# Attention scores of six batches on four 64 by 64 squares of TensorE instead of two 128 by 64 halves

## Chip, cores and metric

The kernel runs on one core of a Trainium2 chip (trn2). The metric is the device time of one execution in microseconds (us); lower is better. The time before is the median of three runs.

## What is computed

Windowed causal attention with a linear position bias, and behind it a bilinear feed-forward layer over all tokens:

```python
# q, k, v: (8, 8, 576, 64); w_a, w_b: (512, 1536); w_out: (1536, 512); float32
scores = q @ k.T / sqrt(64)                    # per batch and head
mask = (rel >= 0) & (rel < 128)                # rel = query position - key position
scores = where(mask, scores - slope[head] * abs(rel), -1e9)
attn = softmax(scores) @ v
x = attn with heads joined                     # (8 * 576, 512)
out = ((x @ w_a) * (x @ w_b)) @ w_out
```

## The kernel before

Everything is float32 outside; inside, each large product is made of float16 halves. A value x becomes hi = fp16(x) and lo = fp16(x - hi), and a product of two such values is three float16 matmuls (hi hi, hi lo, lo hi) that add up in PSUM. The feed-forward layer takes most of TensorE's time: up (w_a and w_b; line 941 of the helper `terms`) and down (w_out; line 1102), as matmuls of 128 rows by 128 columns of the array with 288 columns streamed. From the third batch on it multiplies blocks by a seven-product scheme.

While the feed-forward of one batch runs, the attention of the next is woven into it. `attention()` (a generator) makes one step per pair of heads, 4 pairs per batch (p = 0 to 3), and yields seven times in a step; `Pace` advances it along the feed-forward steps. TensorE's order is written out by this weave and is kept; the orders of the other engines are set by the scheduler that builds the program. Pairs p = 2 and 3 fall into the up phase of the feed-forward, p = 0 and 1 into the down phase.

**Scores.** Queries go in 9 tiles of 64. Tile i needs 64, 128 or 192 keys (64 for tile 0, 128 for tile 1, 192 for the other seven). Batch 0 and batch 1 make their scores in float32 (lines 646 and 445). For the batches 2 to 7 (six of them, 24 pairs of heads) `lay_out_qk` first sends four copies from SBUF to SBUF: `qst` gets q-hi in partitions 0 to 63 and q-lo in 64 to 127, and then k-hi and k-lo are doubled into both partition halves, over the place of q. `scores` (line 449) then makes, per tile and head, two matmuls over 128 partitions: qst times k-hi (hi hi + lo hi) and qst times k-lo (hi lo + lo lo). The two heads of the pair sit in the two column halves of the array (PSUM partitions 0 to 63 and 64 to 127). The profile writes this shape as 128*64.

**Banks.** `BANKS` puts the 9 tiles into four PSUM banks of 512 columns, 3 + 2 + 2 + 2 tiles, each 384 columns wide in all. They come from the pool `ps_at`, which has 3 banks in rotation and also serves the attention's second product (`pv`, `x_ps`, line 575, 42 matmuls in 128*64, two banks) and small sums (`qtot`, `vtot`). A step calls `scores` for banks 0 and 1 together, then bank 2, then bank 3.

**Behind a bank.** Per tile VectorE adds the bias and takes the row minimum (line 454, which reads PSUM), ScalarE takes the exponential (line 455). `normalize` later makes reciprocals of the sums (467, 468) and writes the normalised probabilities as hi (ScalarE, 471) and lo (VectorE, 472) into `phl`. A transposing DMA makes `pT` of it, which `pv` reads one or two steps later. `keep_x` (488) moves the result of `pv` to SBUF, `split_x` (509, 510) makes halves of it for the feed-forward.

## Time and profile before

| | |
|---|---|
| median of the runs | 968.81 us (968.03 to 969.47) |
| the profiled execution's own time | 967.01 us |
| its span, first to last instruction | 965.2 us |
| TensorE busy | 951.8 us, 9304 matmuls |
| VectorE, ScalarE, GpSimd busy | 723.0, 636.7, 260.7 us |
| granted TensorE clock | 0.998 of 2.4 GHz |

The profiled execution is 1.80 us under the median. Busy time of TensorE counts a matmul from its start to a modelled end; successive matmuls overlap, so the distance between two starts says what a matmul takes in a stream. In the timeline a row joins equal instructions that follow each other: its first number is the start of the first, its second the time to the end of the last.

### The profile page before, as it was taken

Reading aid. Unit: us, or ns where it says so; the run is one execution under the profiler, and the core shown is the slowest. Engines: PE = TensorE matmul, PEld = TensorE weight load, DVE = VectorE, ACT = ScalarE, POOL = GpSimd, SP = SyncE. Lnnn points to the kernel's source line nnn. Section 1 sums busy time; section 2 is a strip of 40 time slices with the busy share of each in tenths; the row PEclk is TensorE's granted clock in tenths of the full one; section 3 lists DMA queues with packets and bytes.
Section 4 is the critical chain, followed back from the end, with each engine's and each line's share of the span. In section 5 each row is a group of like instructions: output and inputs, shape, how many; then the busy total and the mean of one; then the engine's idle time right before and its main releaser. Section 6 shows DMA issues by size and latency. Waiting matters only on the chain.

```text
span 965.2 us, 23861 instructions
## 1 busy us (share of the span) xinstructions
PE 951.8 (99%) x9304; PEld 743.2 (77%) x9305; DVE 723.0 (75%) x2004; ACT 636.7 (66%) x1725; POOL 260.7 (27%) x307
## 2 busy tenths in 40 slices
PE   8989999999999999999999999999999999999998
PEld 6667777777877777777877777777777777877776
DVE  7999997578888768887876677767676676589860
ACT  6877787577776666776766766767667666424531
POOL 1211222045546123632432122401222112311110
PEclk9999999999999999999999999999999999999999
DMA  9373745626437333464246452473245441210001
GB/s 357 144 271 106 261 83 127 163 85 120 89 92 173 76 69 70 108 165 94 45 100 178 88 114 50 101 190 82 57 95 111 137 75 39 51 38 7 2 7 43
DMA packets 148433, 102.83 MB, mean 107 GB/s; under 512 B 120032, under 2 KB 128352, under 8 KB 147296
## 3 DMA queue, kind: packets, MB, share of 16 engines
q1 hardware_dynamic: 138816, 91.77, 38.7%
q10 hardware_dynamic: 9504, 9.54, 3.1%
q8 instruction: 73, 1.20, 0.5%
q14 instruction: 40, 0.33, 0.1%
HBM read 48.33 MB, written 9.44 MB: 60 GB/s over the span
## 4 chain that ended last, share of the span: by engine, by line
PE 84%; DVE 6%; ACT 4%; DMA 3%; issue 1%; SPq 1%; ACTq 0%; POOL 0%; DVEq 0%
PE dn_ps L1102 22%; PE ch L941 19%; PE up_ps L941 15%; PE p L941 14%; PE x_ps L575 4%; PE sc_ps L449 4%; PE dch L1127 2%; PE d L1127 1%; DMA v<-in_vP 1%; DMA qk<-in_kT 1%; DVE wsum L146 1%; ACT t L455 1%; DMA wdn<-in_w_b 1%; ACT vsq L341 1%; PE sc_ps L445 1%
## 5 line engine op out<-in xcount | busy, mean ns | idle before, releaser
L941 PEld LDWEIGHTS <-wup 128*128 128x128 f16 x3072 | 296.1, 98 | 83.9 <-issue 7.9
L1102 PE MATMUL dn_ps<-h,wdn 128*128 128x288 f16 x1728 | 218.4, 286 | 0.0
L1102 PEld LDWEIGHTS <-wdn 128*128 128x128 f16 x1728 | 165.8, 98 | 44.7
L941 PE MATMUL up_ps<-xr,wup 128*128 128x288 f16 x1536 | 195.5, 286 | 2.2 <-DVE v L704 1.1
L941 PEld LDWEIGHTS <-wsum 128*128 128x128 f16 x1152 | 111.7, 98 | 30.9 <-issue 1.3
L1056 POOL TENSOR_TENSOR xr<-xr,row 128x288 f32<-128x288 f32 x64 | 63.0, 985 | 265.7 <-DVE row L1054 234.0
L455 ACT ACTIVATE t<-t,mn 128x192 f32<-128x192 f32 (+2 forms) x252 | 107.2, 427 | 25.7 <-DVE mn L454 25.4
L472 DVE SCALAR_TENSOR_TENSOR phl<-t,rin,phl 128x192 f16<-128x192 f32 (+2 forms) x252 | 103.8, 453 | 17.7 <-ACT phl L471 17.6
L941 PE MATMUL ch<-xr,wup 128*128 128x288 f16 x768 | 115.0, 286 | 0.3 <-DVE xr L1061 0.3
L941 PE MATMUL p<-xr,wup 128*128 128x288 f16 x768 | 115.1, 286 | 0.0
L941 PE MATMUL ch<-xr,wsum 128*128 128x288 f16 x768 | 111.5, 286 | 0.4 <-ACT xr L1026 0.4
L471 ACT ACTIVATE phl<-t,rin 128x192 f16<-128x192 f32 (+2 forms) x252 | 88.9, 425 | 30.3 <-DVE rin L468 15.7
L933 ACT CAST h<-xr 128x576 f16<-128x576 f32 x84 | 56.0, 667 | 46.9 <-DVE xr L1061 23.2
L454 DVE CUSTOM_DVE_ANT_0 t<-sc_ps,bias,neg 128x192 f32<-128x192 f32 (+2 forms) x216 | 73.7, 390 | 10.7 <-PE sc_ps L449 10.6
L934 DVE TENSOR_TENSOR h<-xr,h 128x576 f16<-128x576 f32 x78 | 61.5, 790 | 24.6 <-ACT h L933 24.2
L510 DVE TENSOR_TENSOR xr<-v,xr 128x576 f16<-128x576 f32 x52 | 48.8, 951 | 24.2 <-ACT xr L509 24.1
L430 POOL TENSOR_SCALAR bias<-rel_sb,ninv,sl_sb 128x192 f32<-128x192 f32 x24 | 22.5, 936 | 148.5 <-DVE mn L454 125.0
L1038 ACT ACTIVATE row<-ch,g 128x288 f32<-128x288 f32 x64 | 31.8, 497 | 45.3 <-PE ch L941 45.3
L941 PE MATMUL p<-xr,wsum 128*128 128x288 f16 x384 | 57.5, 286 | 0.0
L455 ACT ACTIVATION_READ_ACCUMULATOR t<-t,mn 128x1 f32 x252 | 47.5, 189 | 0.0
L504 POOL TENSOR_TENSOR xq<-xq,sq 128x576 bf16<-128x576 bf16 x21 | 29.0, 1379 | 66.2 <-ACT sq L503 66.2
L1061 DVE SCALAR_TENSOR_TENSOR xr<-xr,g,ch 128x288 f32<-128x288 f32 x64 | 32.6, 510 | 15.0 <-PE ch L941 15.0
(193 smaller groups left out, 1497.7 us busy)
## 6 DMA issues: line engine op xcount, KB each, us to landing
v<-in_vP SPq DMA_DIRECT2D x8, 1280.0 KB, 6.3
qk<-in_qT SPq DMA_DIRECT2D x28, 288.0 KB, 4.0
qk<-in_kT SPq DMA_DIRECT2D x28, 288.0 KB, 4.4
out<-row ACTq DMA_DIRECT2D x56, 144.0 KB, 2.4
wdn<-in_w_a SPq DMA_DIRECT2D x12, 512.0 KB, 5.2
wdn<-in_w_b SPq DMA_DIRECT2D x12, 512.0 KB, 6.0
wdn<-in_w_out SPq DMA_DIRECT2D x12, 512.0 KB, 5.0
qst<-qkh SPq DMA_DIRECT2D x24, 144.0 KB, 2.8
```

The lines of the kernel that those rows point to most:

```text
L449: pe.matmul(ps[64 * e:64 * e + 64, c:c + w], o.qs[:, e, qq], ks[:, e, kk], start=not last, stop=last)
L454: beside[1] = vec.tensor_tensor_reduce(out=t[:, c:c + w], in0=ps[:, c:c + w], in1=o.bias[:, WIN - w:WIN], scale=-0.125 if o.b == 1 else o. ...
L455: beside[0] = act.activation(t[:, c:c + w], t[:, c:c + w], AF.Exp, bias=o.mn[:, n:n + 1], scale=-1.0, accum_out=o.sm[:, n:n + 1])
L471: beside[0] = last_phl[0] = act.activation(phl[:, 0, pc:pc + w], e, AF.Copy, scale=s)
L472: beside[1] = vec.scalar_tensor_tensor(out=phl[:, 1, pc:pc + w], in0=e, scalar=s, in1=phl[:, 0, pc:pc + w], op0=ALU.mult, op1=ALU.subtract)
L510: vec.tensor_tensor(out=xs[:, n, 1, :, :], in0=src, in1=xs[:, n, 0, :, :], op=ALU.subtract)
L575: last = pe.matmul(xp[oc // 512][64 * h:64 * h + 64, o0:o0 + w], vt[0:rows, c:c + 64], probs(pt, rows, blocks, h), start=(n == 0 and first ...
L933: act.copy(h[:, f, :, 0, :], hid)
L934: eng.tensor_tensor(out=h[:, f, :, 1, :], in0=hid, in1=h[:, f, :, 0, :], op=ALU.subtract)
L941: pe.matmul(ps[:, 0:HT], w[:, wi, k, :], xs[:, b, xi, k, :], start=(first and n == 0), stop=(last and n == len(ks) - 1), skip_group_check= ...
L1056: pool.tensor_tensor(out=x0, in0=x0, in1=mid, op=ALU.mult)
L1102: pe.matmul(ps[:, 0:HT], wdn[:, f, wi, e * P:(e + 1) * P], h[:, f, t, hi, :], start=(m == 0 and n == 0), stop=(m == NF - 1 and n == 2))
```

## The change

`BANKS` no longer serves the batches 2 to 7. `FOLDED` puts their 9 tiles into two groups of two banks. A group's first bank is computed in the upper half of the array's rows (partitions 0 to 63 of the operands), its second bank in the lower half (64 to 127), each head in its column half as before, so four squares of 64 by 64 hold a matmul each. `in_turn` orders the two banks' matmuls by the columns that each half has been given so far. Per tile and head there are three matmuls (hi hi, lo hi, hi lo); lo lo is no longer computed. The copies change with it: the row half that holds q gets k-hi and k-lo of the keys 0 to 319 beside it, the half that holds k gets q-hi and q-lo of the queries 320 to 575, and nothing is overwritten. A step calls `score_pair` twice, where banks 0 and 1, and bank 2, stood; `pv` of p = 0 and 3 moves behind the next yield; for p = 2 `normalize` runs once over nine tiles.

```diff
--- before.py
+++ after.py
@@ -40,6 +40,24 @@
 
 BANKS = (((0, 0), (1, 128), (8, 256)), ((2, 0), (3, 320)), ((4, 0), (5, 320)), ((6, 0), (7, 320)))
 NCOL = 2048
+
+
+FOLDED = ((((2, 0), (1, 192), (0, 320)), ((5, 0), (6, 320))), (((3, 0), (4, 320)), ((7, 0), (8, 320))))
+FOLD = 320
+
+
+def in_turn(g):
+
+    ends, todo, out = [0, 0], [[(i, c, n) for i, c in FOLDED[g][half] for n in range(3)] for half in range(2)], []
+    while any(todo):
+        half = min((h for h in range(2) if todo[h]), key=lambda h: ends[h])
+        i, c, n = todo[half].pop(0)
+        out.append((half, i, c, n))
+        ends[half] += TILES[i][1]
+    return out
+
+
+ORDER = [in_turn(g) for g in range(2)]
 PRIO = 2000
 SEVEN = B - 1
 
@@ -413,11 +431,10 @@
 
 
         b, p, hi, lo, sc = o.b, o.p, o.kh, o.kl, o.sc
-        o.qs = work.tile([P, 2, S], F16, tag="qst", name="qst", bufs=1)
-        sp.dma_start(o.qs[0:64, :, :], hi[0:64, :, :])
-        sp.dma_start(o.qs[64:128, :, :], lo[0:64, :, :])
-        sp.dma_start(hi[0:64, :, :], hi[64:128, :, :])
-        sp.dma_start(lo[0:64, :, :], lo[64:128, :, :])
+        o.other = work.tile([P, 2, 2, FOLD], F16, tag="qst", name="qst", bufs=1)
+        for n, x in enumerate((hi, lo)):
+            sp.dma_start(o.other[0:64, n, :, :], x[64:128, :, 0:FOLD])
+            sp.dma_start(o.other[64:128, n, :, 0:S - FOLD], x[0:64, :, FOLD:S])
 
         t = small.tile([P, 1], F32, tag="ninv", name="ninv")
         vec.scalar_tensor_tensor(out=t, in0=sc[:, 0:1], scalar=-8.0, in1=sc[:, 1:2], op0=ALU.mult, op1=ALU.mult)
@@ -444,10 +461,10 @@
                         r = slice(64 * e, 64 * e + 64)
                         pe.matmul(ps[r, c:c + w], o.q[r, qq], o.k[r, kk], start=True, stop=True)
                 continue
-            for ks, last in ((o.kh, False), (o.kl, True)):
-                for e in range(2):
-                    pe.matmul(ps[64 * e:64 * e + 64, c:c + w], o.qs[:, e, qq], ks[:, e, kk], start=not last, stop=last)
-        for i, c in BANKS[bi]:
+        minima_of(o, BANKS[bi], ps, t, ready)
+
+    def minima_of(o, tiles, ps, t, ready):
+        for i, c in tiles:
             pc, w = TILES[i]
             n = o.n
             with tc.issue_after(ready.ins) if ready else ExitStack():
@@ -455,6 +472,22 @@
             beside[0] = act.activation(t[:, c:c + w], t[:, c:c + w], AF.Exp, bias=o.mn[:, n:n + 1], scale=-1.0, accum_out=o.sm[:, n:n + 1])
             o.parts.append((n, t[:, c:c + w], pc, w))
             o.n += 1
+
+    def score_pair(o, g, ready=None):
+
+        banks_of = [(ps_at.tile([P, 512], F32, tag="at", name="sc_ps"), work.tile([P, 512], F32, tag="t", name="t", bufs=4)) for _ in range(2)]
+        order = ORDER[g]
+        for half, i, c, n in order:
+            w = TILES[i][1]
+            qq, kk = slice(64 * i, 64 * i + 64), slice(64 * i + 64 - w, 64 * i + 64)
+            r = slice(64 * half, 64 * half + 64)
+            mine, other = (o.kh, o.kl), o.other
+            a, z = ((0, 0), (1, 0), (0, 1))[n]
+            for e in range(2):
+                qx, kx = (mine[a][r, e, qq], other[r, z, e, kk]) if half == 0 else (other[r, a, e, 64 * i - FOLD:64 * i + 64 - FOLD], mine[z][r, e, kk])
+                pe.matmul(banks_of[half][0][64 * e:64 * e + 64, c:c + w], qx, kx, start=(n == 0), stop=(n == 2))
+        for half, (ps, t) in enumerate(banks_of):
+            minima_of(o, FOLDED[g][half], ps, t, ready)
 
     def normalize(o):
 
@@ -785,8 +818,10 @@
             if two == 2 and p == 1:
                 with behind():
                     nxt = squares(i + 1)
-            for bi in range(two if o else 0):
-                scores(o, bi, nxt.ready if two == 2 and p == 1 and nxt else None)
+            if o and two == 2:
+                score_pair(o, 0, nxt.ready if p == 1 and nxt else None)
+            elif o:
+                scores(o, 0)
             if two == 1 or p != 1:
                 with behind():
                     nxt = squares(i + 1)
@@ -815,24 +850,22 @@
             if p != 2:
                 split(nxt, p != 3)
             yield i + 3 / 7
-            if o:
+            if o and two == 2:
+                score_pair(o, 1)
+            elif o:
                 scores(o, 2)
             if p == 3 and nxt and nxt.b > 1:
                 low_qk(nxt, beside[1])
-            if prev and p not in (1, 2):
+            if two == 1 and prev and p not in (1, 2):
                 pv(prev.p, st, prev, prev.vhl)
-            if two == 2 and p in (1, 3):
-                if p == 2:
-                    with behind():
-                        normalize(o)
-                scores(o, 3)
             yield i + 4 / 7
+            if two == 2 and prev and p not in (1, 2):
+                pv(prev.p, st, prev, prev.vhl)
             if p == 2:
                 prev.vhl = split_v(st, prev.p)
-                if two == 1 or p not in (1, 3):
-                    with behind():
-                        normalize(o)
-            if o and (two == 1 or p not in (1, 3)):
+                with behind():
+                    normalize(o)
+            if o and two == 1:
                 scores(o, 3)
             lay_out(nxt)
             load(i + 2)
@@ -844,7 +877,7 @@
                 for k, _ in enumerate(split_x(st, b - 1 <= 3, b - 1 >= 2)):
                     yield i + (4.2 + 0.2 * k) / 7
             yield i + 5 / 7
-            if o:
+            if o and o.parts:
                 with behind():
                     normalize(o)
             if p == (0 if b == 1 else 1):
```

TensorE, second run of scores of pair p = 0 in the first batch whose scores follow this path (sc_ps are the PSUM tiles, qst the copies, qkh and qkl the hi and lo halves). Before:

```order
L449 LDWEIGHTS qst_2233
L449 MATMUL sc_ps_2486<-qkh_2028,qst_2233 64x192
L449 LDWEIGHTS qst_2233
L449 MATMUL sc_ps_2486<-qkh_2028,qst_2233 64x192
L449 LDWEIGHTS qst_2233
L449 MATMUL sc_ps_2486<-qkl_2029,qst_2233 64x192
L449 LDWEIGHTS qst_2233
L449 MATMUL sc_ps_2486<-qkl_2029,qst_2233 64x192
```

The same place in the changed kernel:

```order
L488 LDWEIGHTS qkh_2028
L488 MATMUL sc_ps_2496<-qst_2233,qkh_2028 64x192
L488 LDWEIGHTS qkh_2028
L488 MATMUL sc_ps_2496<-qst_2233,qkh_2028 64x192
L488 LDWEIGHTS qst_2233
L488 MATMUL sc_ps_2498<-qkh_2028,qst_2233 64x192
L488 LDWEIGHTS qst_2233
L488 MATMUL sc_ps_2498<-qkh_2028,qst_2233 64x192
L488 LDWEIGHTS qkl_2029
L488 MATMUL sc_ps_2496<-qst_2233,qkl_2029 64x192
L488 LDWEIGHTS qkl_2029
L488 MATMUL sc_ps_2496<-qst_2233,qkl_2029 64x192
```

Before, one bank is filled, and each weight load and matmul stands twice, once per head; now two banks take turns, two heads each, with the operands' places exchanged between the row halves.

ScalarE, in an up phase of the seven-product scheme, pair p = 2 (t are the exponentials, phl the normalised probabilities, ch and p the feed-forward's PSUM tiles, xr and row what they are copied to). Before:

```order
L1038 ACTIVATE row<-ch,g 128x288
L1044 COPY xr<-p_8686 128x288
L467 ACTIVATE rin<-sm 128x7
L471 ACTIVATE phl<-t,rin 128x64
L471 ACTIVATE phl<-t,rin 128x128
L471 ACTIVATE phl<-t,rin 128x192 x5
L933 CAST h<-xr 128x2x288
L455 ACTIVATE t,sm<-t,mn 128x192 x2
L1026 COPY xr<-ch 128x288
```

The same place in the changed kernel:

```order
L472 ACTIVATE t,sm<-t,mn 128x192 x4
L1071 ACTIVATE row<-ch,g 128x288
L1077 COPY xr<-p_8964 128x288
L500 ACTIVATE rin<-sm 128x9
L504 ACTIVATE phl<-t,rin 128x192
L504 ACTIVATE phl<-t,rin 128x128
L504 ACTIVATE phl<-t,rin 128x64
L504 ACTIVATE phl<-t,rin 128x192 x6
L966 CAST h<-xr 128x2x288
L1059 COPY xr<-ch 128x288
```

Before, seven tiles are normalised and two exponentials follow ahead of the next copy of ch; now four exponentials stand ahead, and nine tiles are normalised in one piece.

## Rows read from the trace of the kernel before

**Rows 1.** The page's first part: busy time of each engine and its share of the span.
```profile
span 965.2 us, 23861 instructions
PE 951.8 (99%) x9304; PEld 743.2 (77%) x9305; DVE 723.0 (75%) x2004; ACT 636.7 (66%) x1725; POOL 260.7 (27%) x307
```
**Rows 2.** The page's chain that ended last, by engine.
```profile
PE 84%; DVE 6%; ACT 4%; DMA 3%; issue 1%; SPq 1%; ACTq 0%; POOL 0%; DVEq 0%
```
**Rows 3.** Timeline of TensorE, banks 0 and 1 (p = 0): start, length, engine, line, shapes.
```profile
608.62 0.90 PE L1102 MATMUL dn_ps<-h,wdn 128*128 128x288 f16 x6
609.45 0.22 PE L449 MATMUL sc_ps<-qkh,qst 128*64 128x64 f16 x2
609.50 0.20 PE L449 MATMUL sc_ps<-qkl,qst 128*64 128x64 f16 x2
609.53 0.23 PE L449 MATMUL sc_ps<-qkh,qst 128*64 128x128 f16 x2
...
609.65 0.25 PE L449 MATMUL sc_ps<-qkh,qst 128*64 128x192 f16 x2
...
610.06 0.25 PE L449 MATMUL sc_ps<-qkl,qst 128*64 128x192 f16 x2
610.24 4.58 PE L1102 MATMUL dn_ps<-h,wdn 128*128 128x288 f16 x36
```
**Rows 4.** Timeline of TensorE, p = 0: bank 2 with pv, then bank 3 alone.
```profile
614.69 3.10 PE L1102 MATMUL dn_ps<-h,wdn 128*128 128x288 f16 x24
...
618.07 1.51 PE L575 MATMUL x_ps<-pT,vhl 128*64 128x128 f16 x42
619.52 2.38 PE L1102 MATMUL dn_ps<-h,wdn 128*128 128x288 f16 x18
...
622.28 5.32 PE L1102 MATMUL dn_ps<-h,wdn 128*128 128x288 f16 x42
```
**Rows 5.** Timeline of TensorE around banks 2 and 3 of p = 1.
```profile
635.96 3.10 PE L1102 MATMUL dn_ps<-h,wdn 128*128 128x288 f16 x24
...
639.77 5.44 PE L1102 MATMUL dn_ps<-h,wdn 128*128 128x288 f16 x43
```
**Rows 6.** Timeline of TensorE around banks 0, 1 and vtot of p = 2.
```profile
649.34 0.90 PE L941 MATMUL ch<-xr,wup 128*128 128x288 f16 x6
...
651.07 0.90 PE L941 MATMUL p<-xr,wup 128*128 128x288 f16 x6
```
**Rows 7.** Timeline of TensorE around a pv that runs alone.
```profile
679.88 0.90 PE L941 MATMUL ch<-xr,wsum 128*128 128x288 f16 x6
680.71 1.54 PE L575 MATMUL x_ps<-pT,vhl 128*64 128x128 f16 x42
682.18 0.91 PE L941 MATMUL p<-xr,wsum 128*128 128x288 f16 x6
```
**Rows 8.** Timeline of TensorE around bank 2, pv and bank 3 of p = 3.
```profile
700.20 0.90 PE L941 MATMUL ch<-xr,wup 128*128 128x288 f16 x6
...
703.16 0.91 PE L941 MATMUL p<-xr,wup 128*128 128x288 f16 x6
```
**Rows 9.** Timeline of TensorE, a bank of batch 1: float32 in two squares.
```profile
133.08 0.17 PE L112 MATMUL wtot<-c,ones 128*128 128x1 bf16 x1
133.18 0.87 PE L445 MATMUL sc_ps<-qkl,qkh 64*64 64x192 f32 x8
133.98 1.03 PE L941 MATMUL up_ps<-xr,wup 128*128 128x288 f16 x7
```
**Rows 10.** TensorE's waits: line waited for, us in total, times, longest us.
```profile
PE sc_ps L449 <- DVE mn L454: 0.6, 1, 0.6
...
PE ch L941 <- ACT xr L1026: 0.4, 2, 0.2
```
**Rows 11.** ScalarE's groups by shape: count, busy us, mean ns, idle before.
```profile
L455 ACT ACTIVATE t<-t,mn 128x192 f32<-128x192 f32 x196 | 86.9, 445 | 11.5 <-DVE mn L454 11.4
L471 ACT ACTIVATE phl<-t,rin 128x192 f16<-128x192 f32 x196 | 73.6, 442 | 10.9 <-DVE rin L468 10.9
```
**Rows 12.** The page's DMA issues: KB each, us from issue to landing.
```profile
qst<-qkh SPq DMA_DIRECT2D x24, 144.0 KB, 2.8
...
qkl<-qkl SPq DMA_DIRECT2D x24, 144.0 KB, 2.5
```

## Prediction

> **What bounds the kernel.** I read the page's first part, then the chain that ended last, then the timeline of TensorE around each kind of attention work, then its waits. The first shows TensorE busy for 99% of the span and the next engine for 75% [rows 1]. The chain is 84% TensorE [rows 2]. That it passes through other engines for the rest stops the stream little: the waits of the scores and of the seven products' ch, the two that matter below, are 0.6 and 0.4 us in the whole kernel [rows 10]. So time taken out of TensorE's stream comes out of the total, as long as no new wait opens.
>
> The timeline gives each stop of the feed-forward a price: from the start of its last matmul before to that of the first behind, less one normal step. That step is 0.12 us, from 36 matmuls in one row: (4.58 - 0.29) / 35 [rows 3], where 0.29 is the length of one. Banks 0 and 1 (20 matmuls): the last one before starts at 608.62 + 0.90 - 0.29 = 609.23, the next at 610.24, so 1.01 - 0.12 = 0.89 us [rows 3]. In it, two heads start together and a pair of 192 columns takes (610.06 - 609.65) / 5 = 0.082 us, pairs of 128 and 64 take two thirds and one third of it, 0.056 and 0.028 (0.12 for two pairs up to 609.65, 0.03 up to 609.53). That makes 6 x 0.082 + 2 x 0.056 + 2 x 0.028 = 0.66; the other **0.22 us** is the passage into the other shape and back. The same way:
> - p = 0: bank 2 with pv 1.90, bank 3 alone 0.55 [rows 4] (0.55 = 4 x 0.082 + 0.22, the same passage)
> - p = 1: banks 2 and 3 in one piece 0.88 [rows 5]
> - p = 2: banks 0, 1 and vtot 1.00 [rows 6]; banks 2 and 3 apart, 2 x 0.55
> - p = 3: bank 2, pv and bank 3 in one piece 2.23 [rows 8]
> - a pv alone 1.57 [rows 7]
>
> Per batch, with 0.89 for banks 0 and 1 of p = 0, 1, 3: 3.34 + 1.77 + 2.10 + 3.12 = **10.33 us** in ten stops, and six batches follow this path.
>
> **The change, part by part.** *Matmuls.* Each pair of heads makes 54 instead of 36, but with four squares streaming at once a run of two banks needs only the longer of its two row halves: first run 3 pairs each of 192, 128 and 64 columns (0.25 + 0.17 + 0.09 = 0.50 us) beside 6 of 192 (0.49); second run 6 of 192 on both sides, 0.49. With the passage a run is 0.72 us. Eight runs: 5.76. vtot stays behind its run: 1.00 - 0.89 = 0.11. *pv.* In p = 0 and 3 it leaves the scores' stop and pays its own passage: 2 x 1.57 = 3.14. Together 9.01 us in ten stops. Saved: 10.33 - 9.01 = 1.32 per batch, **7.9 us** in six. The passages cancel (ten stops before, ten now), so all of it is streaming: in widths of 192, a pair of heads streams 16 steps before and 12 now, and 24 x 4 x 0.082 is again 7.9.
>
> *The first steps of a run.* No row shows four squares being filled. The lower row half starts after the upper one has had its loads; between nothing and one narrow step (0.03 us, [rows 3]) per run, 48 runs: 0 to 1.4 us. I take the middle, **+0.6**, since the two heads' loads in the rows share their time almost wholly but never came from two row halves.
>
> *Copies.* Four DMAs before and four now, on the same queue, but 288 KB instead of 576 (the row halves need 320 and 256 of 576 columns) and without a second pair that waits for the first to land. Before, that chain was two landings, 2.8 and then 2.5 us [rows 12]. Scores read them three sevenths of a step later; they become earlier, worth nothing, as nothing waited for them.
>
> *Banks of PSUM.* A run takes two of the pool's three banks at once. Both were used by an earlier run or pv with several microseconds of feed-forward between, and today a score bank was waited for once in the whole kernel, 0.6 us [rows 10]. pv of p = 0 and 3 now takes the first score bank of the run 18 to 24 feed-forward matmuls later (2.2 to 2.9 us); before, bank 3 of p = 3 took bank 2's place in the rotation after the 1.57 - 0.22 = 1.35 us of pv [rows 7], without a wait. So I cost this at nothing; the one wait may go (-0.6).
>
> *ScalarE and VectorE.* The same minima, exponentials and normalised tiles in larger pieces: four tiles at once instead of two and two, and for p = 2 nine tiles normalised in a row. In the up phase the copy of ch, on which TensorE's next product on that bank waits, stands behind them. Before: 7 normalised tiles and 2 exponentials ahead of it, now 9 and none. With 0.44 each [rows 11] that is about 4 us in both. TensorE waits for this copy twice today, 0.4 us in all [rows 10]. I take **+0.4** over the kernel, from nothing to 0.9 per batch (two more tiles at 0.44 uncovered).
>
> *Moved later:* pv, keep_x and split_x of p = 0 by some 2.2 us; the feed-forward reads their result from the up phase on, 649.34 - 618.07 = 31 us later [rows 4, 6]. *Two reciprocals less* per batch: hidden.
>
> **Sum.** -7.9 + 0.6 + 0.4 = -6.9 us against the profiled execution's 967.01: 960.1. That execution is 1.8 us under the median, so for a median: 968.81 - 6.9 = **961.9 us**, 0.7% less. A measurement of this kernel tells a change from none at about 0.2%, 1.9 us.
>
> **Rivals.**
> 1. *The row halves do not stream together* where they share columns. Every square of one column half would then follow the other: a run takes 15 or 12 steps, 1.00 or 0.98 us in place of 0.50 or 0.49, 48 x 0.49 = +23.5, so 968.81 - 7.9 + 23.5 = **984.4 us, slower**. It decides as soon as a third of the second half's time is not shared (7.9 / 23.5). Against it: in batch 1 two squares in different row halves and different column halves fill one bank with eight float32 matmuls of 192 columns within 0.80 us [rows 9]; one float32 column costs about two float16 ones there, 0.16 us a matmul, so one after another they would need 1.3. For it: squares that share their columns never occur in this trace. Chance 0.08.
> 2. *Starts become the limit.* 60 instructions must be issued in 0.50 us. The tightest the rows show is a pair of 64 columns, two loads and two matmuls, in 0.03 us [rows 3]; at that rate 30 matmuls need 0.42 us and fit. If the two starts of a pair were free only because they lie in one row half, and each start cost the 0.028 of such a pair, runs would take 0.84 and 0.67: 24 x (0.34 + 0.18) = +12.5, **973.4 us**; halfway between, no gain at all. Chance 0.06. The Trainium skill, "TensorE: Matmul & The Clock Gate", section "Wait — 56ns, not 53.3ns?", has a rule of this kind: two matmul starts are never closer than about 25 ns. By that figure, as an estimate, the runs would take 0.75 and 0.60 us and the kernel 969.4 us, no change. The trace speaks against it, with starts of two heads in one row of the timeline and a pair every 0.03 us.
> 3. *The larger pieces on ScalarE and VectorE make TensorE wait* in p = 2 and 3, the upper bound above: 0.9 x 6 = 5.4 instead of 0.4, **966.9 us**. For it: nine tiles normalised without a copy of the feed-forward between. Against: today's list ahead of that copy is as long and costs 0.4 us. Chance 0.10.
>
> That the change does not do what it says can be left out: the order of TensorE's instructions shows both banks taking turns in each of the 48 runs.
>
> **How the numbers follow.** My forecast has 0.76. Its own bounds: 7.9 - 0 and the one wait gone, 968.81 - 8.5, less the runs' half spread of 0.7: 959.6; above, the late starts at 1.4 and half of the third rival's price, 2.7: 968.81 - 7.9 + 4.1 + 0.7 = 965.7, taken as 966.0, which leaves out the first two rivals and part of the third, under 0.2. Faster by over 0.2%: 0.76 and half of the third rival, 0.81. Within: the rest of the third and half of the second, 0.08. Slower: the first and half of the second, 0.11.
>
> **What would show it.** Right: in the timeline a run of scores stops the feed-forward for 0.70 to 0.75 us, matmuls start in fours with 0.082 us from four to four, pv alone stays at 1.57, the waits' table is no longer than today. Wrong: fours that are 0.16 us apart (first rival), starts evenly spread by 0.02 us or more (second), or new rows in the waits' table with ch or a score bank waiting for ScalarE or VectorE (third).

## The result and the profile after: slower, with the streaming as forecast

The changed kernel takes **980.82 us** (median of 4 runs, 979.98 to 982.04) against 968.75 for the kernel before on the same chip: ratio 1.0126, 95% interval 1.0108 to 1.0143. The forecast was 961.9 us, within 959.6 to 966.0. The profiled execution's span is 978.2 us, 13.0 more than before.

The page of the kernel after, its first part and the engines of its chain; they answer to [rows 1, 2]:

```profile
span 978.2 us, 24700 instructions
...
PE 949.1 (97%) x9737; PEld 739.2 (76%) x9737; DVE 729.8 (75%) x1998; ACT 636.2 (65%) x1719; POOL 259.7 (27%) x307
...
PE 74%; DVE 10%; ACT 7%; issue 3%; DMA 3%; POOL 1%; SPq 0%; ACTq 0%; DVEq 0%; POOLq 0%
```

TensorE is busy 2.7 us less in a span that is 13 us longer, and the chain passes through TensorE for 74% instead of 84%, through VectorE and ScalarE for 17% instead of 10%. The stream (the matmuls in their order) got shorter, and it stands still more often.

**The stream.** The timeline of TensorE at the first run of p = 0, the counterpart of [rows 3] (start, length, engine, line, shapes):

```profile
623.43 0.90 PE L1135 MATMUL dn_ps<-h,wdn 128*128 128x288 f16 x6
624.26 0.27 PE L488 MATMUL sc_ps<-qst,qkh 64*64 64x192 f16 x2
624.27 0.27 PE L488 MATMUL sc_ps<-qkh,qst 64*64 64x192 f16 x2
624.37 0.24 PE L488 MATMUL sc_ps<-qst,qkl 64*64 64x192 f16 x2
624.37 0.25 PE L488 MATMUL sc_ps<-qkh,qst 64*64 64x192 f16 x2
...
624.73 0.20 PE L488 MATMUL sc_ps<-qst,qkl 64*64 64x64 f16 x2
...
624.89 1.89 PE L1135 MATMUL dn_ps<-h,wdn 128*128 128x288 f16 x14
```

Two heads of the upper row half start at 624.26, two of the lower at 624.27, and the next four 0.10, then 0.08 us later. The stop is 624.89 - (623.43 + 0.90 - 0.29) - 0.12 = 0.73; over the trace the 18 runs of 30 matmuls cost 0.72 each, the 24 of 24 cost 0.715, those with vtot 0.834, a pv alone 1.56. With the medians of each kind, the stops of six batches take 24 x 0.715 + 18 x 0.7205 + 6 x 0.834 + 12 x 1.5615 = 53.9 us. In the trace before the same sum over its own kinds is 18 x 0.8865 + 18 x 0.5475 + 6 x (2.2245 + 1.8915 + 1.0005 + 0.8765) = 61.8. That is 7.9 less, the forecast's term to the digit.

**The waits.** TensorE's waits after (line waited for, us in total, times, longest us):

```profile
PE n_ps L623 <- POOL xq L537: 4.5, 1, 4.5
PE ch L974 <- ACT xr L1059: 3.1, 7, 1.0
PE ch L974 <- DVE xr L1094: 2.2, 3, 1.0
...
PE up_ps L974 <- DVE xr L987: 2.0, 1, 2.0
PE up_ps L974 <- ACT xr L985: 1.7, 2, 0.9
...
PE ch L974 <- DVE xr L1082: 1.4, 1, 1.4
...
PE dn_ps L1135 <- DVE h L967: 0.9, 1, 0.9
```

Before, ch waited 0.4 us for this ScalarE copy [rows 10]; n_ps (the small sums over the squares of x, from which the scale of the hidden layer is made) waited for nothing. Summed over the stream, the time that stops and steps take beyond the median of their kind is 28.5 us after and 10.2 before: **18.3 us of new waits**. Where noise is told from a wait is a choice in this sum; other choices give 17 to 19. With a stretch at the lower clock behind the longest of them (2.3 us, below), 7.9 less and 20.6 more make 12.7 of the 13.0. A count without that choice agrees: from start to start of the feed-forward's matmuls, the stops of scores and pv take 7.5 us less than before and everything else 20.5 more.

The longest wait, in the timeline of TensorE after:

```profile
289.63 1.39 PE L1135 MATMUL dn_ps<-h,wdn 128*128 128x288 f16 x10
295.52 0.64 PE L623 MATMUL n_ps<-xq,ones 128*128 128x512 bf16 x2 [4.50 <-POOL xq L537]
295.97 5.39 PE L1135 MATMUL dn_ps<-h,wdn 128*128 128x288 f16 x24
```

What GpSimd, which n_ps waited for, did until then, in its timeline after:

```profile
286.11 0.87 POOL L447 TENSOR_SCALAR bias<-rel_sb,ninv,sl_sb 128x192 f32<-128x192 f32 x1 [12.14 <-DVE mn L471]
286.96 2.26 POOL L291 TENSOR_TENSOR wsum<-wup 128x512 f32<-128x512 f16 x2
...
294.20 1.27 POOL L537 TENSOR_TENSOR xq<-xq,sq 128x576 bf16<-128x576 bf16 x1
```

and the same place on GpSimd in the kernel before:

```profile
283.68 1.28 POOL L504 TENSOR_TENSOR xq<-xq,sq 128x576 bf16<-128x576 bf16 x1 [1.11 <-ACT sq L503]
284.94 1.98 POOL L430 TENSOR_SCALAR bias<-rel_sb,ninv,sl_sb 128x192 f32<-128x192 f32 x1
```

Before, the sum xq stands ahead of the bias of the next heads. After, pv and with it the square of x come later, and in the built order of GpSimd's queue the bias stands first. It waits 12.14 us for VectorE's minima to free its buffer, and the side sums of the weights (wsum), which stand behind it, start at 286.96. The input of xq comes at 289.27 (the square started at 288.59 and took 0.68), when the bias is done; from then on xq stands behind the side sums, and it is added at 294.20. TensorE had nothing left to do from 291.02. An estimate from these rows, which no run shows: had xq kept its old place ahead of the bias, it would have been done at 289.27 + 1.27 = 290.54, before TensorE came to n_ps. The 24 matmuls behind the wait take 5.39 us where 24 take 3.10 in [rows 4].

### The profile page after: what moved, and what is told of

Same layout as the page of the kernel before. It is cut to its first block, busy times and chain, and to the rows that moved or that the text cites. A ratio compares the mean times of both kernels' runs of the same rounds, so it can differ in the third digit from the quotient of the medians.

```text
span 978.2 us, 24700 instructions
## 1 busy us (share of the span) xinstructions
PE 949.1 (97%) x9737; PEld 739.2 (76%) x9737; DVE 729.8 (75%) x1998; ACT 636.2 (65%) x1719; POOL 259.7 (27%) x307
## 4 chain that ended last, share of the span: by engine, by line
PE 74%; DVE 10%; ACT 7%; issue 3%; DMA 3%; POOL 1%; SPq 0%; ACTq 0%; DVEq 0%; POOLq 0%
PE dn_ps L1135 18%; PE ch L974 16%; PE up_ps L974 13%; PE p L974 12%; PE x_ps L608 4%; PE dn_ps L936 3%; PE sc_ps L488 2%; ACT phl L504 2%; PE dch L1160 2%; DMA v<-in_vP 2%; PE sc_ps L462 1%; PE d L1160 1%; DMA qk<-in_kT 1%; DVE t L471 1%; DVE phl L505 1%
## 5 line engine op out<-in xcount | busy, mean ns | idle before, releaser
L1135 PE MATMUL dn_ps<-h,wdn 128*128 128x288 f16 x1728 | 221.0, 288 | 0.9 <-DVE h L967 0.9
L1089 POOL TENSOR_TENSOR xr<-xr,row 128x288 f32<-128x288 f32 x64 | 61.8, 966 | 248.2 <-DVE row L1087 219.7
L505 DVE SCALAR_TENSOR_TENSOR phl<-t,rin,phl 128x192 f16<-128x192 f32 (+2 forms) x252 | 109.7, 484 | 13.2 <-ACT phl L504 12.8
L543 DVE TENSOR_TENSOR xr<-v,xr 128x576 f16<-128x576 f32 x52 | 50.9, 994 | 25.9 <-ACT xr L542 25.7
L1066 DVE TENSOR_TENSOR xr<-p,xr 128x288 f32<-128x288 f32 x64 | 29.0, 453 | 26.3 <-PE p L974 16.0
L608 PEld LDWEIGHTS <-vhl 128*64 128x64 f16 x1176 | 39.9, 110 | 6.8 <-issue 6.4
```

Source lines behind the costliest of these rows:

```text
L505: beside[1] = vec.scalar_tensor_tensor(out=phl[:, 1, pc:pc + w], in0=e, scalar=s, in1=phl[:, 0, pc:pc + w], op0=ALU.mult, op1=ALU.subtract)
L543: vec.tensor_tensor(out=xs[:, n, 1, :, :], in0=src, in1=xs[:, n, 0, :, :], op=ALU.subtract)
L608: last = pe.matmul(xp[oc // 512][64 * h:64 * h + 64, o0:o0 + w], vt[0:rows, c:c + 64], probs(pt, rows, blocks, h), start=(n == 0 and first ...
L1089: pool.tensor_tensor(out=x0, in0=x0, in1=mid, op=ALU.mult)
L1135: pe.matmul(ps[:, 0:HT], wdn[:, f, wi, e * P:(e + 1) * P], h[:, f, t, hi, :], start=(m == 0 and n == 0), stop=(m == NF - 1 and n == 2))
```

## The experiments

Theories from the trace after: **A**, pv of p = 0 and 3 stands too late; **B**, the larger pieces on ScalarE and VectorE; **C**, the squares or their copies; **D**, that the other engines' queues, which work in order, were laid out with TensorE's old order, so that moving a piece either way opens waits. All times are medians in us; the kernel before on the same chip stands in brackets, then the interval of the ratio to it. There are 17 experiments.

**1 to 4: the parts of the change alone.** Experiment 1 puts pv back behind the second run, in the same stop:

```diff
-            if two == 1 and prev and p not in (1, 2):
+            if prev and p not in (1, 2):
                 pv(prev.p, st, prev, prev.vhl)
             yield i + 4 / 7
-            if two == 2 and prev and p not in (1, 2):
-                pv(prev.p, st, prev, prev.vhl)
```

> The changed kernel with pv of p = 0 and 3 back at its old place, right behind the second run of scores and ahead of the yield. Theory A (the new waits come from pv being late, and with it the copies, squares and halves of x that hang on it): the waits of about 20 us go and the 7.9 us of streaming remain, 961 to 966 us. Theory B (they come from scores in two large pieces, four or five minima in a row on VectorE and larger normalising bursts): the waits stay, 976 to 983 us; pv also finds the first of its two banks taken by scores and may wait up to 1 us in each of 12 places.

Experiment 2 makes the reverse of this edit in the kernel before.

> The kernel before (128 by 64 scores, four banks at their old places) with pv of p = 0 and 3 alone moved behind the yield. Passages alone: 12 more at 0.22 us, +2.6, 971.4 us. Theory A: on top of that most of the 20 us of waits, 980 us or more. Theory B: 970 to 973 us.

Experiment 3 is the kernel before with banks 2 and 3 always in one run and the minima and normalised tiles in the change's pieces; experiment 4 adds the late pv to it. Experiment 4 is thus the change without its squares:

```diff
-                score_pair(o, 1)
+                for bi in (2, 3):
+                    scores(o, bi)
```

> 128 by 64 scores and the old copies, but called in the two pieces of the changed kernel (banks 0 and 1, then 2 and 3 together), one normalising of nine tiles in p = 2, pv at its old place. Passages alone: 12 fewer, -2.6, 966.2 us. Theory A: 965 to 969 us. Theory B: 980 us or more. If neither piece matters and the waits come from the squares' own copies and order: 966 us as under A, but e4 is then near 969 as well.

> Everything of the changed kernel but the squares: 128 by 64 scores and the old copies, two pieces per step, pv late. Passages as before, so 968.8 us without waits. Theories A and B: both pieces are there, 985 to 991 us (the changed kernel's 980.8 plus the 7.9 us of streaming). Theory C (squares, their copies or their third term make the waits): 967 to 971 us.

Measured: 976.78 [969.49; 1.0059 to 1.0089], 978.87 [969.49; 1.0081 to 1.0119], 977.08 [969.49; 1.0057 to 1.0091], 986.85 [969.49; 1.0159 to 1.0189]. Waits of experiment 1:

```profile
PE x_ps L608 <- DVE mn L471: 6.3, 7, 1.7
PE ch L972 <- ACT xr L1057: 2.1, 6, 0.6
```

Experiment 2 has the change's longest wait, in the kernel before:

```profile
PE n_ps L590 <- POOL xq L504: 3.2, 2, 2.2
```

Experiment 4 has that and the waits of ch:

```profile
PE n_ps L627 <- POOL xq L541: 3.7, 2, 3.4
...
PE ch L980 <- ACT xr L1065: 1.9, 6, 0.4
PE ch L980 <- DVE xr L1100: 1.7, 3, 0.8
PE ch L980 <- ACT row L1077: 1.6, 4, 0.7
```

C falls: without squares and their copies the change costs 17.4 us, with them 12.1, so they give back about 5 (the ratios are 1.0174 and 1.0126). The waits of n_ps and ch come with the moves alone. A late pv costs 9.4, of which 2.6 are two more passages per batch (12 x 0.22); larger pieces cost 7.6 although they save as many passages. Putting pv back wins about 5 us of the change's 12 and opens a new wait: x_ps now takes a score bank whose minima are still being read, 6.3 us in seven waits. Neither A nor B gives all four times: experiment 1 lies in B's range, 2 just under A's, 3 between the two, 4 in the range that both share.

**5 to 7: moves the other way.** Experiment 5 asks for the scale of the hidden layer, and with it n_ps, later:

```diff
             if p == 1 and b > 1:
+                hidden_scale(st)
                 st = load_v(b)
...
-            if prev and p == 0:
+            if prev and p == 0 and i == n:
                 hidden_scale(st)
```

> The changed kernel with hidden_scale (two matmuls on the squares of x, n_ps, for which TensorE waits 4.5 us once on GpSimd's sum xq and runs at the lower clock for 2.4 us behind it) moved from the end of p = 0 to behind the first run of scores of p = 1, some 3 us later. Theory A (pv and what hangs on it is late): that wait and the clock's fall shrink or go, 973 to 978 us. Theory B (large pieces): GpSimd is as late by more than the 3 us, or the wait turns up elsewhere; 979 to 982.

Experiments 6 and 7 put pv of p = 0 and 3 earlier, two sevenths into the step, in the change and in the kernel before (the call at its former place goes; the lines show the new place):

```diff
             yield i + 2 / 7
+            if two == 2 and prev and p not in (1, 2):
+                pv(prev.p, st, prev, prev.vhl)
```

> The changed kernel with pv of p = 0 and 3 moved to the other side: a yield ahead of the second run of scores instead of a yield behind it, in one stop with qtot. Passages 12 fewer than in the changed kernel where it joins qtot only by a step (as x_ps with qtot today, 1.60): no change of streaming. Theory A: what hangs on pv becomes early, the waits go, 961 to 967 us, less 0.6 us for each p = 0 in which the transposed probabilities land later than pv now starts (up to 3.6 us in six). Theory B: pieces stay as large, 974 to 981. Theory D (any move in TensorE's order makes the others' orders worse): 974 to 985.

> The kernel before with the same single move of pv, to the yield ahead of bank 2. Passages alone +2.6 us, 971.4. Theory A: 969 to 974 (earlier is harmless but for the transposed probabilities, as in the run above). Theory D: 976 or more, as when pv alone was made late (978.9).

Measured: 991.9 [969.94; 1.0206 to 1.0279], 986.49 [969.94; 1.0161 to 1.0203], 993.39 [969.94; 1.0227 to 1.0257]. Waits of experiment 5, where n_ps still waits 0.9 us:

```profile
PE ch L975 <- ACT xr L1060: 6.8, 8, 1.8
PE vtot L368 <- DVE vc L364: 3.6, 2, 2.6
...
PE n_ps L623 <- POOL xq L537: 0.9, 1, 0.9
```

Of experiment 6, where the scale of the next q and k is late:

```profile
PE qtot L417 <- DVE both L409: 10.2, 5, 2.8
```

And of experiment 7, where scores wait for the copies of q and k:

```profile
PE sc_ps L449 <- DMA qkh<-qkh: 7.8, 7, 1.9
```

A falls as a matter of lateness: in the otherwise unchanged kernel before, the one call of pv costs 23.5 us when it stands earlier (experiment 7) and 9.4 when it stands later (experiment 2). Asking later shortens n_ps's wait from 4.5 to 0.9 us, and vtot and ch wait instead. Each move makes other rows wait, as D says; experiment 7 lies in D's range, 5 and 6 lie above all of theirs.

**8 to 10: the squares in the old places.** Experiment 8 leaves the squares and undoes the moves: the second run of p = 0 is cut in two halves (tiles 3 and 7, then 4 and 8) that stand where banks 2 and 3 stood, and pv follows in the same stop, its last 64 columns in spare columns of a score bank. Only p = 2 keeps the whole second run.

```diff
-                score_pair(o, 1)
+                score_pair(o, 1, None, 0 if p == 0 else None)
...
+                pv(prev.p, st, prev, prev.vhl, o.banks[0][0][:, 192:256] if two == 2 else None)
             yield i + 4 / 7
...
+            elif o and p == 0:
+                score_pair(o, 1, None, 1)
```

> The change with its four squares, put back into the stops of the kernel before as far as they go: for p = 0 the second run is cut into two halves (tiles 3 and 7, then 4 and 8) that stand where banks 2 and 3 stood, pv of p = 0 and 3 follows the first half (p = 0) or the whole run (p = 3) without a yield between, its 64 last columns in spare columns of a score bank. Only p = 2 keeps its second run in one piece, with the nine tiles normalised in a row. Stops per batch from measured pieces: p = 0 0.72 + 1.82 (1.90 with 0.25 in place of 0.33) + 0.47, p = 1 2 x 0.72, p = 2 0.83 + 0.72, p = 3 0.72 + 2.18: 8.90 in place of 10.33, 8.6 us in six batches. Theory D (what costs is that work moved in TensorE's order, against queues that were laid out with the old places): 961 to 966 us, and the waits list as short as before. Theory A and B as fixed prices of a late pv and of larger pieces: both mostly gone here as well, 962 to 964. Against both, that any other schedule costs 10 us or more, whatever is moved: 970 to 985 us, with long waits for GpSimd, VectorE or ScalarE in batches 1 to 3.

Experiment 9 is the change with xq summed on VectorE, experiment 10 both:

```diff
-            pool.tensor_tensor(out=st.xq, in0=st.xq, in1=sq, op=ALU.add)
+            vec.tensor_tensor(out=st.xq, in0=st.xq, in1=sq, op=ALU.add)
```

> The change with one thing more: the sum xq of the squares of x (three of four heads' pairs in each of seven batches, 21 instructions of 1.4 us) is added on VectorE instead of GpSimd, where in batch 2 it stood behind a bias that waited 12 us and behind the side sums, and let n_ps wait for 4.5 us. If that queue made the wait, n_ps does not wait there, TensorE keeps its higher clock behind it, and 4.9 + 2.4 us come back, less what 21 adds of some 0.6 us on VectorE push: 973 to 977 us. If GpSimd was only named and the wait comes from further back (squares of x late on ScalarE, pv late), n_ps still waits, for VectorE or ScalarE: 979 to 983.

> Both edits, the four squares in the old stops and the sum xq on VectorE: a version meant to beat both kernels. Theory D: within 2 us of the old stops alone if no n_ps waits there, else better by that wait; 960 to 966 us. If any new schedule costs: 970 or more.

Measured: 980.39 [969.29; 1.0093 to 1.0128], 975.83 [1.0043 to 1.0077], 972.66 [1.0020 to 1.0047]. In 9, n_ps waits nowhere and the kernel is 5 to 6 us faster than the change (expected: 973 to 977): GpSimd's queue did make that wait. A part of it comes back in another row, which the change did not have:

```profile
PE qtot L417 <- DVE both L409: 2.8, 1, 2.8
```

Experiment 8 gains nothing on the change and falls into the range set down for "any other schedule costs 10 us or more". Its waits:

```profile
PE sc_ps L612 <- DVE mn L471: 6.3, 7, 1.5
PE ch L978 <- ACT xr L1063: 4.0, 8, 1.3
```

The first row is the price of the spare columns: they lie in a bank whose minima VectorE is reading, and pv's matmuls into it wait for that. With xq on VectorE besides (experiment 10) the row of ScalarE shrinks from 4.0 to 1.5 us, though that edit moves nothing on TensorE. Experiment 10 too ends in its range for the case that any new schedule costs, 970 or more.

**11 to 14: two repeated waits.** Experiment 11 issues pv ahead of the run of its stop, so that the spare columns are written before any minimum is read, and normalises the nine tiles of p = 2 as seven and two. Experiment 12 is the same with the second run of p = 0 whole.

```diff
-                    normalize(o)
+                    normalize(o, 7)
...
+        keep = ahead(o.banks[0][0][:, 192:256]) if ahead else None
         tiles = [x if part is None else x[part:part + 1] for x in FOLDED[g]]
```

> The version with old stops and xq on VectorE, with its two repeated waits taken out. (1) In p = 0 and 3 pv is issued ahead of the score run of the same stop, so that its last columns go into the spare columns of a score bank before any minimum of that bank is read: the trace of the version before lets pv wait there for the minima seven times, 1.17, 0.97, 1.26, 0.30, 1.13, 0.32 and 0.32 us, 5.5 in all. (2) For p = 2 the nine tiles are normalised in two pieces, seven and two, as in the kernel before, instead of in a row: ch waits for ScalarE and VectorE 0.55 + 0.30 us per batch behind that run. If these waits have these causes, they go: 972.7 - 5.5 - 0.85 x 4 = 963.8, so 963 to 966 us, faster than both kernels. If any new order opens about as many waits as it closes: 969 to 976, with waits in other rows.

> The same, but the second run of p = 0 is not cut: pv and the whole run stand in one stop, 2.18 us, and the stop of the other half (0.47) goes away. Streaming and passages: 1.82 + 0.47 = 2.29 becomes 2.18, 0.1 us per batch, 0.6 less. Theory B (larger pieces on VectorE and ScalarE make TensorE wait): four minima at once with keep_x of x before them, 2 to 4 us more than the cut version, 966 to 968. Theory D: within 3 us of the cut version either way, by chance of the queues.

Experiment 13 takes the seven and two back; 14 leaves xq on VectorE only in the first three of its batches.

```diff
-            vec.tensor_tensor(out=st.xq, in0=st.xq, in1=sq, op=ALU.add)
+            (vec if added[0] <= 9 else pool).tensor_tensor(out=st.xq, in0=st.xq, in1=sq, op=ALU.add)
```

> Old stops, xq on VectorE, pv ahead of the score run in p = 0 and 3, but the nine tiles of p = 2 normalised in a row again. This undoes one of two edits of the run before last, which took 5.5 us of pv's waits away and opened about 2.6 us per batch of waits of ch for VectorE and ScalarE in batches 4 to 6. If the pieces of seven and two opened them: ch waits 0.55 + 0.30 per batch as with old stops, and 972.7 - 5.5 = 967.2, so 966 to 968.5. If pv's new place opened them (keep_x of x now ahead of the minima): they stay, 970 to 972.

> The same, with xq on VectorE only in the three batches in which GpSimd also makes the side sums, and on GpSimd in the other four, 12 adds of some 0.6 us less on VectorE. If VectorE's load is what ch waits for in batches 4 to 6, 1 to 4 us better than the run above: 963 to 967. If it is the order of VectorE's and ScalarE's queues and not their load, the same within 1.5 us.

Measured: 970.91 [968.92; 1.0013 to 1.0032], 971.20 [968.92; 1.0008 to 1.0032], 973.36 [969.44; 1.0025 to 1.0055], 974.64 [969.44; 1.0041 to 1.0074]. In all four pv's wait for the minima, 5.5 us in experiment 10, is gone, and ch waits more. The waits of ch in experiment 13:

```profile
PE ch L983 <- ACT row L1080: 2.1, 3, 1.1
...
PE ch L983 <- DVE xr L1091: 1.3, 3, 0.4
```

The same rows in experiment 14:

```profile
PE ch L986 <- ACT row L1083: 3.2, 4, 1.4
...
PE ch L986 <- DVE xr L1094: 2.1, 3, 0.9
```

With four batches of adds taken off VectorE, ch waits longer for VectorE (2.1 instead of 1.3), not less. So **VectorE's load** is not what these waits follow; ScalarE's was not varied. 13 is no better than 11, so the seven and two had not opened them. They had closed one: ch waits 0.4 us for ScalarE's copy in 11 and 1.5 in 13. That pv's new place had opened the others is what is left of 13's expectation, though its time lies above both of that expectation's ranges. 11 and 12 agree within their intervals: whole or cut, the run's size in p = 0 does not matter either.

**15 to 17: one place at a time.** Experiment 15 keeps pv ahead in p = 0 alone, with the nine tiles in a row; 16 normalises them as five and four; 17 also issues the loads of q and k of p = 3 ahead of the four copies on SP's queue.

```diff
-                    normalize(o)
+                    normalize(o, 5 if two == 2 else 9)
```

```diff
+            if first_load:
+                load(i + 2)
             lay_out(nxt)
-            load(i + 2)
+            if not first_load:
+                load(i + 2)
```

> Old stops, xq on VectorE, pv ahead of the score run in p = 0 only; in p = 3 it stands behind the run again, as in the first version with old stops. The waits of pv for the minima in p = 0, 0.97, 1.26, 1.13, 0.32 and 0.32 us, go; those of p = 3, 1.17 and 0.30, come back; the two waits that the last runs had 30 matmuls behind the run of p = 3 (0.60 per batch, ch for VectorE) and 0.8 to 1.3 per batch in p = 2 should go, if pv ahead in p = 3 opened the first and pv ahead in p = 0 not the second. If both go: 972.7 - 4.0 = 968.7, no change against the kernel before. If the waits in p = 2 stay (they would then belong to pv ahead in p = 0): 970 to 972.

> The same with the nine tiles of p = 2 normalised as five and four, one seventh of a step apart, instead of in a row. If it is the length of that piece on ScalarE which ch waits for (0.55 + 0.30 us per batch from batch 4 on, more in batches 2 and 3), these waits go: 3 to 4 us better than the run above, 965 to 968.5, and the first version that beats both kernels. If it is the order of the queues, waits of the same size come elsewhere, and the time stays within 1.5 us.

> The version with the nine tiles as five and four, and the loads of q and k for p = 3 issued ahead of the four copies of p = 2 on SP's queue instead of behind them. In the version before, ch waits three times for a row of ScalarE that stands behind the squares of q and k, which wait 1.63 us for the load of k: 3.5 us in all. Its load lands at 652.10, after the copies, while in the kernel before it lands at 649.57, issued among the copies. If this place on SP's queue is the cause, the three waits shrink to under 0.5 us each and the time is 2 to 3.5 us under the version before, 963 to 965 us. Against it: the copies land some 1.3 us later, and the scores of p = 2 then wait for them: 966 to 970, with waits of sc_ps for DMAs of qst.

Measured: 971.02 [969.76; 1.0005 to 1.0029], **966.71 [969.76; 0.9963 to 0.9985]**, 975.17 [969.85; 1.0034 to 1.0073]. Waits of experiment 15:

```profile
PE ch L985 <- ACT row L1082: 2.9, 3, 1.8
...
PE ch L985 <- ACT xr L1070: 1.5, 5, 0.4
...
PE ch L985 <- DVE xr L1105: 1.2, 2, 0.9
```

Of experiment 16:

```profile
PE ch L985 <- ACT row L1082: 3.5, 3, 1.8
...
PE ch L985 <- ACT xr L1070: 0.4, 2, 0.2
...
PE ch L985 <- DVE xr L1105: 0.3, 1, 0.3
```

And of experiment 17:

```profile
PE sc_ps L493 <- DMA qst<-qkh: 6.0, 4, 2.2
PE sc_ps L493 <- DMA qst<-qkl: 2.9, 4, 1.9
...
PE ch L989 <- ACT row L1086: 0.6, 1, 0.6
```

15 shows that pv ahead in p = 3 had opened the wait for VectorE 30 matmuls behind it: the row of 1.3 us that 13 has for VectorE is gone. In 16, five and four in place of nine close the wait for ScalarE's copy (1.5 to 0.4, what the kernel before has [rows 10]) and VectorE's (1.2 to 0.3). The kernel before has for VectorE:

```profile
PE ch L941 <- DVE xr L1061: 0.3, 1, 0.3
```

That these waits go is what the expectation of 16 sets down for the length of the nine tiles' piece on ScalarE as the cause, so of B this much stands. Experiment 16 beats both kernels: 3.05 us under the one before, ratio 0.9974. This rests on 10 runs against 19; the two traced executions (967.07 us and, before, 967.01) do not show it. In those traces the stops of scores and pv take about 7 us less than before and everything else about 7 more. No run has the edits other than the squares (xq on VectorE, five and four) in the kernel before, so how much of the 3.05 us is the squares' is not shown. The last long row of 16, 3.5 us in three waits, can be followed in ScalarE's timeline at the longest of them:

```profile
652.17 1.16 ACT L406 ACTIVATE qkl<-qk 128x1152 bf16<-128x1152 f32 x1 [1.63 <-DMA qk<-in_kT]
...
654.93 0.48 ACT L1082 ACTIVATE row<-ch,g 128x288 f32<-128x288 f32 x1
```

The row that ch waits for stands behind squares of q and k that wait for a load, and the load stands behind the copies on SP's queue. 17 tests that: with the loads first the row falls from 3.5 to 0.6 us, and the scores wait 8.9 us for the copies, which puts the time above both expected ranges. The cause was right, the remedy was not.

## Why the prediction was wrong

**Right: streaming, passages, starts.** A run of 0.72 us, 7.9 us saved in six batches, pv alone at 1.57: all as forecast. The first rival would show fours 0.16 us apart; they are 0.08 apart. The second would show evenly spread starts; four lie within 0.01 us (624.26 and 624.27), and 30 matmuls take no longer than their streaming. (Halfway, that rival's own sum gives 967.2 us, 1.6 of gain and not none.) The Trainium skill's rule that the second rival's text names ("TensorE: Matmul & The Clock Gate", section "Wait — 56ns, not 53.3ns?": starts no closer than about 25 ns) is not borne out for matmuls in different squares, four of which start here within those 0.01 us. The term of +0.6 for the late lower row half was nothing that a run's 0.72 leaves room for.

**Wrong: "as long as no new wait opens".** The sum took this condition from the short waits' table [rows 10] and then priced its breach at +0.4. The trace after shows 18.3 us of new waits. A table of waits tells what waits now, not how little separates the others from waiting. Three steps carry it:
- *"Moved later: pv, keep_x, split_x of p = 0"*, costed at nothing because the feed-forward reads x 31 us later. That is not the next reader. The square of x and the sum xq are read by n_ps two sevenths of a step behind pv's new place, through GpSimd's queue, where the bias went ahead of it. In the batch with side sums this cost 4.5 us and 2.3 at the lower clock; experiment 9, which takes xq out of that queue, got 5 to 6 us back. I chose a batch without side sums for the row.
- *"ScalarE and VectorE +0.4"*, the third rival at most 0.9 per batch. The rows of ch alone sum to 6.7 us (3.1 + 2.2 + 1.4) where 0.7 stood before (0.4 + 0.3), and the mechanism of that rival, nine tiles in a row in p = 2, is real: experiment 16 closes its waits, 2.0 us of what experiment 15 had. But the 4 us of work ahead of the copy of ch that I compared were equal before and after. That it matters instead when they come, and in how long a piece, fits experiment 16; it is not shown for the other waits of ch. Experiment 14 shows that VectorE's load does not set them.
- *"Banks of PSUM ... at nothing"*, by the rotation. In the change itself that held. In the nearest variants it did not: with pv in the same stop it waits 6.3 us for the minima (experiments 1 and 8). The old places could not have been kept for free either.

**What the runs show in its place.** Experiments 2, 3, 4 and 7 open waits of this kind in the kernel before, without a single square: 2 by moving pv back, 7 by moving it ahead. 15 to 17 each close one row by one place and, in 17, open another. So the cost follows from where TensorE's pieces stand against in-order queues on the other engines and on SP, not from the squares or their copies. The price of the moves was 17.4 us without the squares (experiment 4) and, by the sum 12.1 + 7.9, about 20 with them, against 7.9 saved. With most places restored, xq on VectorE and the nine tiles in two pieces, experiment 16 is 3 us faster than the kernel before.

Left open: the other engines' order is set when the kernel is built, so a move on TensorE changes the queues as well. No run held those queues fixed while TensorE's order changed, and how much of each wait comes from the new place and how much from the re-laid queue stays open; for the wait of n_ps, the estimate above speaks for the queue. The waits of up_ps in the trace after (2.0 and 1.7 us) are followed by no experiment. Nor is it settled what the long wait in p = 2 of experiments 11 to 16 has to do with pv ahead in p = 0. No run brings the second run of p = 2 back to two stops.

## What to carry to other kernels

Where one engine is busy for 99%, price a change first by its stream and then by the slack of every value that the engine will meet at a new time: follow each moved result through the in-order queue of each engine between it and its next reader, in the batch where that queue is fullest. Make the saving in the old places first and move nothing else; here the kernel with the squares was 12 us slower with the new places, and 3 us faster once most of the old places were back and two rows of waits had been closed by edits of their own. A row in the waits' table that closes when a piece moves is only half of the reading: look which row has grown.

## What was not expected of the hardware

- In and behind the wait of 4.5 us the granted clock was at the lower of its two levels (1.2 of 2.4 GHz). It fell at 293.8 us, while TensorE had stood still since 291.0, and rose at 300.6, when TensorE had been busy again since 295.5. In that stretch a normal step was about 0.22 us (5.39 / 24) instead of 0.12. Three windows, before, within and after it (length, then busy time and instructions of PE, PEld, DVE, ACT and POOL, granted clock, DMA share, GB/s):

```profile
288.00:291.40 3.40, 3.02 (x25) 2.27 (x24) 2.01 (x2) 1.83 (x4) 3.40 (x5) 1.00 0.49 136
296.20:300.70 4.50, 4.50 (x20) 2.79 (x19) 4.43 (x10) 0.86 (x2) 3.68 (x5) 0.51 0.00 0
301.00:305.00 4.00, 4.00 (x59) 3.11 (x58) 3.24 (x16) 3.94 (x15) 0.00 (x0) 1.00 1.15 213
```

  So this wait of 4.5 us cost another 2.3 behind it (5.39 - 3.10), half of its own length. The 2.4 us that the expectations of experiments 5 and 9 name are this loss, not the length of the stretch.
- Four squares that share rows and columns pairwise stream at once: 24 matmuls of 192 columns take 0.715 - 0.22 = 0.49 us, six times the 0.082 us from four to four.
- A run followed at once by pv takes 2.18 us (experiment 1, in the stops where pv waits for nothing) where the two apart take 0.715 + 1.56 = 2.28: of the passage of 0.22, only 0.10 is saved when a run of squares meets a run of half columns.
